# A cached-attention kernel: six batches of x loaded plainly and transposed on TensorE, the other x loads placed behind K loads, constant matmuls at the start, two heads of wq issued by ScalarE

## The chip, the cores and the metric

The kernel runs on one core of a Trainium2 chip. A core has a matrix engine (TensorE, PE in the profile, with PEld for its weight loads), three engines for elementwise work (VectorE or DVE, ScalarE or ACT, GpSimd or POOL), a queue engine (SyncE or SP) that issues transfers, and 16 DMA engines that carry them out. The metric is the device time of one execution in microseconds; the number quoted for a kernel is the median of several executions.

## The reference

Two independent problems, A and B, of the same shape, each an attention block with a given K and V cache:

```python
# x [16, 144, 448]   k_cache, v_cache [16, 16, 512, 256]   wq [448, 4096]   wo [4096, 448]
def _A_ref(x, k_cache, v_cache, wq, wo):
    B, Sq, D = x.shape
    H, Dh = 16, 256
    q = (x @ wq).reshape(B, Sq, H, Dh).transpose(0, 2, 1, 3)
    scores = jnp.einsum("bhqd,bhkd->bhqk", q, k_cache) * (Dh ** -0.5)
    p = softmax(scores, axis=-1)
    o = jnp.einsum("bhqk,bhkd->bhqd", p, v_cache)
    return o.transpose(0, 2, 1, 3).reshape(B, Sq, H * Dh) @ wo
```

`reference` returns the results of A and of B side by side in the last axis. All arrays are bf16.

## The kernel before, in words

A *unit* is one head of one batch; there are 256 in A (units 0 to 255) and 256 in B (256 to 511). The first 32 units take two batches in turn (unit U is head U//2 of batch U%2), after that a batch's 16 heads follow each other. Per unit, TensorE does four things: Q = wq' x' (line 1081; two batches at once for most units), S = K Q (line 1112), PV = V' P (line 1168), and its share of the output projection (line 1284), which is cut into pieces of one 128-row chunk of the output times one of 32 slices of wo. A sum over keys goes through a matmul with ones (line 1184). ScalarE computes the exponentials and the reciprocal of the sum, GpSimd and VectorE add up partial sums, VectorE takes Q out of PSUM (1094, 1095) and scales PV into `ring` (1220), from which the projection reads.

**Steps.** The program of each engine is written out unit by unit in one loop over a step i (from line 1472). At step i stand PV of unit i, S of unit i+2 (i+3 from unit 48 on; function `ls`), Q of one unit more (`lq`), and the projection pieces that `op_schedule` gave to that step. At step 44 the lead changes, so two Q's stand in one step, one right after the other. `_Sched.add` puts in the semaphore waits that reads and writes need; every engine runs its own list in order.

**Projection rate.** `op_schedule` hands out pieces by a credit. There are 2.25 pieces per unit (18 chunks of 32 pieces to 256 units). No piece of A comes before step 28 and none of B before step 272 (`OP_START`); the credit grows by `OP_RATE` times 2.25 per step, 1.04 up to step 272 and 1.15 after it.

**Loads.** x must be on chip transposed (`xt_sb`, a ring of `NX` = 6 batches), K transposed (`kt_sb`, a ring of 32 units), V as it is (`v_sb`, a ring of nine pairs of units). The K of the first 48 units is loaded plainly into the V ring (line 1012, 1017) and transposed on TensorE (`t_tr`, line 1032) with evacuations by VectorE and ScalarE (1040). From unit 48 on, K comes in *waves* of 16 units by one transposing DMA (line 988). x comes by transposing DMAs in groups of one to four batches (`X_GROUPS`, line 964). wq, wo, V and stores are plain DMAs (928 and 930, 939, 1002, 1313). Every DMA is issued by SP, in one order. A planner fixes that order ahead of time: `load_list` gives each load the time at which it is used (`clock`, a sum of TensorE costs per step), the step at which its buffer is free, and a duration; the loop after `todo` then picks loads one by one, and prefers other loads to a K wave if they would fall due during it. The `due` step of a load is where its buffer is free, and SP waits there for the engine that frees it.

The pieces that the change and the steps of the prediction touch: `t_init` (line 899), `t_load_wq` (922), `t_load_x` (944), `t_load_k` (979), `t_evac_op` (1295), `op_schedule` (1327), `load_list` (1394), the planner's loop (1424 to 1456), and the step loop (1459 on).

## Time and profile before

| what | us |
|---|---|
| median of 12 executions | 1055.27 (1053.05 to 1056.87) |
| profiled execution, its own time | 1054.66 |
| its span in the trace (first to last instruction) | 1052.8 |
| TensorE busy in the span | 1029.8 |
| VectorE, ScalarE, GpSimd busy | 737.9, 793.6, 634.7 |
| first matmul starts | 3.60 |
| longest idle time of TensorE inside the span | 6.9, at 595.4 |

The profile page gives busy time and idle time by line; "A <- B" after an idle time names the instruction or transfer whose end let A start. A DMA's row in a timeline shows the time that the issuing engine spent on it, not the transfer; the time to landing is told apart. A group of pipelined matmuls is busy a little longer than the distance to the next group: eight matmuls of 144 columns show 0.66 us and the next group begins 0.50 us after them. In sums the distance is used.

### The profile page before, as it was taken

The page shows a single profiled execution, that of the slowest core. Times are in us where ns is not written, and L with a number is a line of the kernel's source. Part 1 is how long each engine was busy: PE and PEld are TensorE (multiplying, and loading weights), DVE is VectorE, ACT ScalarE, POOL GpSimd, SP SyncE. Part 2 cuts the span into 40 slices and gives each one's busy share as a digit, 9 for nine tenths or more (in the row PEclk, how much of TensorE's full clock was granted, in tenths as well). Part 3 has the DMA queues.
Part 4 walks back from the last instruction along what each step waited for, and adds up shares of the span by engine and source line. Part 5 has one row for each costly group of instructions (what it writes and reads, how often), then busy time and mean ns, then how long its engine had stood idle before and what let it go on. Part 6 is the DMA issues. An engine that isn't in the chain of part 4 may idle for free.

```text
span 1052.8 us, 32329 instructions
## 1 busy us (share of the span) xinstructions
PE 1029.8 (98%) x12376; PEld 875.6 (83%) x12376; DVE 737.9 (70%) x2039; ACT 793.6 (75%) x2365; POOL 634.7 (60%) x1030
## 2 busy tenths in 40 slices
PE   6999999999999999999999799999999999999997
PEld 6999888888888888888888688888888888888885
DVE  5776676777777776777776467677776667777775
ACT  5887577777777777777867567787877777788785
POOL 3655556666666666666755456566666666666673
PEclk9999999999999999999999899999999999999999
DMA  9999999999999999999999999999999999999960
GB/s 287 362 340 346 262 303 262 291 290 290 289 290 295 272 260 252 302 289 296 262 290 341 269 268 300 294 268 295 272 275 257 307 249 313 289 274 260 293 205 14
DMA packets 591748, 294.14 MB, mean 279 GB/s; under 512 B 502592, under 2 KB 516768, under 8 KB 591584
## 3 DMA queue, kind: packets, MB, share of 16 engines
q1 hardware_dynamic: 591584, 291.99, 111.0%
q8 instruction: 99, 1.62, 0.6%
q14 instruction: 65, 0.53, 0.2%
HBM read 161.48 MB, written 4.13 MB: 157 GB/s over the span
## 4 chain that ended last, share of the span: by engine, by line
PE 90%; DMA 6%; SPq 1%; ACT 1%; DVE 1%; issue 0%; POOL 0%; ACTq 0%; DVEq 0%
PE s_ps L1112 23%; PE ot_ps L1168 23%; PE qp_ps L1081 22%; PE op_ps L1284 19%; DMA kt_sb<-in_B_k_cache_dram 2%; DMA kt_sb<-in_A_k_cache_dram 2%; PE ot_ps L1184 2%; DMA wq_sb<-in_A_wq_dram 1%; PE qp_ps L1032 1%; PE s_ps L1032 1%; PE qp_ps L1284 1%; ACT rinv_sb L1205 1%; DMA v_sb<-in_B_v_cache_dram 0%; SPq L1002 0%; ACT pt_sb L1122 0%
## 5 line engine op out<-in xcount | busy, mean ns | idle before, releaser
L1132 POOL TENSOR_TENSOR pp_sb<-pt_sb 128x288 f32<-128x288 bf16 x512 | 383.9, 750 | 322.3 <-ACT pt_sb L1122 307.3
L1122 ACT ACTIVATE pt_sb<-s_ps 128x288 bf16<-128x288 f32 x1024 | 364.6, 408 | 183.6 <-PE s_ps L1112 177.3
L1220 DVE TENSOR_TENSOR ring<-ot_ps,rinv_sb 128x288 bf16<-128x288 f32 (+2 forms) x640 | 241.8, 394 | 159.5 <-ACT rinv_sb L1205 154.0
L1112 PE MATMUL s_ps<-qt_sb,kt_sb 128*128 128x144 bf16 x4096 | 341.2, 227 | 8.3 <-DMA kt_sb<-in_B_k_cache_dram 6.9
L1168 PE MATMUL ot_ps<-pt_sb,v_sb 128*128 128x144 bf16 x4096 | 340.7, 226 | 0.4 <-DMA v_sb<-in_B_v_cache_dram 0.4
L1112 PEld LDWEIGHTS s_ps<-qt_sb,kt_sb 128*128 128x128 bf16 x4096 | 288.2, 98 | 60.3 <-issue 7.3
L1205 ACT ACTIVATE rinv_sb<-ln_sb 64x144 f32<-64x144 f32 x928 | 298.2, 321 | 24.4
L1081 PE MATMUL qp_ps<-xt_sb,wq_sb 128*128 128x288 bf16 (+1 forms) x2368 | 302.1, 271 | 2.9 <-DMA wq_sb<-in_A_wq_dram 1.3
L1284 PE MATMUL op_ps<-wo_sb,ring 128*128 128x448 bf16 x1120 | 285.5, 352 | 0.0
L1081 PEld LDWEIGHTS qp_ps<-xt_sb,wq_sb 128*128 128x128 bf16 x2368 | 212.4, 98 | 77.8 <-DVE qt_sb L1094 2.3
L1168 PEld LDWEIGHTS ot_ps<-pt_sb,v_sb 128*128 128x128 bf16 x4096 | 274.7, 98 | 1.2 <-DMA v_sb<-in_B_v_cache_dram 0.6
L1137 POOL TENSOR_TENSOR p_sb<-pp_sb 128x144 f32<-128x144 f32 x464 | 226.6, 488 | 74.3 <-DVE ps_sb L1146 9.5
L1235 DVE TENSOR_REDUCE run_sb<-ot_ps 128x1 bf16<-128x144 f32 x560 | 146.5, 304 | 78.2 <-ACT ln_sb L1192 43.8
L1146 DVE TENSOR_TENSOR ps_sb<-p_sb 64x144 bf16<-64x144 f32 x464 | 156.1, 337 | 45.4 <-POOL p_sb L1137 32.1
L1095 DVE CAST qt_sb<-qp_ps 128x576 bf16<-128x576 f32 x216 | 162.1, 751 | 14.1 <-PE qp_ps L1081 10.5
L1284 PEld LDWEIGHTS op_ps<-wo_sb,ring 128*128 128x128 bf16 x1120 | 93.8, 98 | 20.1
L1192 ACT ACTIVATE ln_sb<-ot_ps 128x144 f32<-128x144 f32 x232 | 67.7, 292 | 33.1 <-PE ot_ps L1184 25.4
L1184 PE MATMUL ot_ps<-ps_sb,ones 128*128 128x144 bf16 x280 | 63.4, 226 | 0.0
L1094 DVE CAST qt_sb<-qp_ps 128x288 bf16<-128x288 f32 x80 | 35.8, 448 | 2.9 <-PE qp_ps L1081 2.6
L1040 ACT ACTIVATE kt_sb<-qp_ps 128x512 bf16<-128x512 bf16 x48 | 29.0, 605 | 6.0 <-PE qp_ps L1032 6.0
L1137 POOL TENSOR_TENSOR ps_sb<-pp_sb 128x144 bf16<-128x144 f32 x48 | 23.4, 488 | 7.3 <-PE ot_ps L1184 0.6
L1184 PEld LDWEIGHTS ot_ps<-ps_sb,ones 128*128 128x128 bf16 x280 | 27.4, 98 | 0.0
(29 smaller groups left out, 153.6 us busy)
## 6 DMA issues: line engine op xcount, KB each, us to landing
v_sb<-in_A_v_cache_dram SPq DMA_DIRECT2D x128, 512.0 KB, 6.9
v_sb<-in_B_v_cache_dram SPq DMA_DIRECT2D x128, 512.0 KB, 7.3
v_sb<-in_A_k_cache_dram SPq DMA_DIRECT2D x22, 512.0 KB, 10.0
out_dram<-ost_sb SPq DMA_DIRECT2D x36, 112.0 KB, 6.2
wo_sb<-in_A_wo_dram SPq DMA_DIRECT2D x8, 448.0 KB, 8.5
wo_sb<-in_B_wo_dram SPq DMA_DIRECT2D x8, 448.0 KB, 8.7
wq_sb<-in_B_wq_dram SPq DMA_DIRECT2D x4, 768.0 KB, 9.8
wq_sb<-in_A_wq_dram SPq DMA_DIRECT2D x3, 768.0 KB, 10.0
```

The source lines that it names most:

```text
L1081: ins = t.matmul(acc, lhsT=wq_sb[:, kc, c0:c0 + 128], rhs=xt_sb[:, kc, xo:xe + 1:max(xe - xo, 1), :], start=(kc == 0), stop=(kc == 3))
L1095: return v.tensor_copy(qt_sb[:, a:b + 1:b - a, :, :], qp_ps[:, :, 0:2 * SQ].rearrange("p e (u q) -> p u e q", u=2))
L1112: ins = t.matmul(s_ps[bank][:, (c % 2) * SQ:(c % 2 + 1) * SQ], lhsT=kt_sb[:, 2 * c + dc, ko:ko + 128], rhs=qt_sb[:, qsl, dc, :], start=(dc ...
L1122: return a.activation(pt_sb[:, psl, 2 * k:2 * k + 2, :].rearrange("p b q -> p (b q)"), s_ps[bank][:, 0:2 * SQ], AF.Exp, scale=DH ** -0.5)
L1132: return g.tensor_tensor(pp_sb[:, :, :], pt_sb[:, psl, 0:2, :], pt_sb[:, psl, 2:4, :], op=ALU.add)
L1137: return g.tensor_tensor(dst, pp_sb[:, 0, :], pp_sb[:, 1, :], op=ALU.add)
L1146: return v.tensor_tensor(ps_sb[p0:p0 + 64, sl, :], p2_sb[0:64, :], p2_sb[64:128, :], op=ALU.add)
L1168: ins = t.matmul(ot_ps[ob][:, dc * SQ:(dc + 1) * SQ], lhsT=v_sb[:, vsl, j, c * DH + dc * 128:c * DH + (dc + 1) * 128], rhs=pt_sb[:, sl, c, ...
L1205: return a.activation(rinv_sb[p0:p0 + 64, sl, :], ln_sb[h0:h0 + 64, :], AF.Exp, scale=-1.0)
L1220: ins = v.tensor_tensor(ring[:, 2 * h:2 * h + 2, r0:r0 + q1 - q0], ot_ps[ob][:, 0:2 * SQ].rearrange("p (c q) -> p c q", c=2)[:, :, q0:q1], ...
L1235: return v.tensor_reduce(run_sb[:, k, j:j + 1], ot_ps[ob][:, 2 * SQ:3 * SQ], axis=AX.X, op=op)
L1284: ins = t.matmul(acc[0:m, 0:D], lhsT=ring[:, c, col0:col0 + m], rhs=wo_sb[:, c, :], start=(c == op_first), stop=(c == op_last))
```

## The change

Six batches of x (A's batches 0 to 5) are no longer loaded by transposing DMAs. Each is loaded plainly as 48 partitions by three rows of 448 (`t_load_xn`) into the last slices of `wo_sb`, which are not yet in use, and transposed by 12 TensorE transposes into the projection's PSUM bank; VectorE and ScalarE copy it from there to `xt_sb` (`t_tr_x`), at steps -4, -3, 20, 21, 23 and 24. The other x loads are in groups of two batches, and the planner puts one directly behind a K wave as soon as its buffer is free. wq of heads 0 and 1 is issued by ScalarE, at the start. TensorE runs 34 matmuls on a constant as its first work. The projection's rate is 1.0 to step 240, 1.35 to step 292, then 1.15. The second Q of step 44 stands behind PV. The planner's durations of K, x and wq loads are changed, as is its first order of loads. The last chunk's evacuation is split between VectorE and ScalarE.

```diff
-    X_GROUPS = ((0, 1), (1, 2), (2, 6), (6, 10), (10, 14), (14, 18), (18, 20), (20, 24), (24, 28), (28, 32))
+    X_GROUPS = tuple((g, g + 2) for g in range(6, NP * Bn, 2))
-    WQ_GROUPS = ((0, 1), (1, 2), (2, 4), (4, 8), (8, 12), (12, 16))
+    WQ_GROUPS = ((2, 4), (4, 8), (8, 12), (12, 16))
+    WARM = 34
-    OP_DELAY, OP_START, OP_RATE = 2, (28, 16), (1.04, 1.15)
-    MARGIN, HOLD = 1.0, 1.0
+    XR, X_AT = 48, {0: -4, 1: -3, 2: 20, 3: 21, 4: 23, 5: 24}
+    OP_DELAY, OP_START, OP_RATE = 2, (28, 16), ((240, 1.0), (292, 1.35), (600, 1.15))
+    MARGIN, HOLD, K_FIX = 1.0, 1.0, 2.4
...
             S.add(ACT, e1, reads=[("scr", 0)], writes=[("scr1", 0)], name="actwarm")
+            t_load_wq(0, 0, 1, ACT)
+            t_load_wq(0, 1, 2, ACT)
...
+            def e3(g):
+                return g.memset(xt_sb[64:128, 3, :, :], 0.0)
+            S.add(DVE, e3, writes=[(("xt", g), g) for g in range(NX)], name="xz")
...
+            def e6(t):
+                ins = None
+                for _ in range(WARM):
+                    ins = t.matmul(op_ps[:, 0:128], lhsT=ones[:, :], rhs=ones[:, :], start=True, stop=True)
+                return ins
+            S.add(PE, e6, reads=[("ones", 0)], writes=[("opp", ("warm", 0))], banks=["op"], name="FAR")
...
+        def x_rows(g):
+            n = SQ // XR
+            c0 = NWO - (NX - g) * n
+            return n, wo_sb[0:XR, c0:c0 + n, :], [(("wo", c // WOG), -1) for c in range(c0, c0 + n)]
+
+        def t_load_xn(g):
+            n, dst, keys = x_rows(g)
+
+            def e(q):
+                return q.dma_start(dst, xs[0][g].rearrange("(t p) d -> p t d", p=XR)).then_inc(sems["xn%d" % g], 16)
+            S.add(SP, e, writes=keys + [(("xn", g), 0)], dma_sem="xn%d" % g, name="xn%d" % g)
+
+        def t_tr_x(g):
+            n, src, keys = x_rows(g)
+            acc = op_ps[:, :].bitcast(BF16)[:, 0:4 * SQ].rearrange("p (c q) -> p c q", c=4)
+
+            def e(t):
+                ins = None
+                for c in range(4):
+                    m = min(128, D - c * 128)
+                    for k in range(n):
+                        ins = t.transpose(acc[0:m, c, k * XR:(k + 1) * XR], src[:, k, c * 128:c * 128 + m],
+                                          ident[0:XR, 0:XR])
+                return ins
+            S.add(PE, e, reads=keys + [(("xn", g), 0), id_key], writes=[("opp", ("x", g))], banks=["op"], name="TX%d" % g)
+
+            def e1(v):
+                return v.tensor_copy(xt_sb[:, 0:3, g, :], acc[:, 0:3, :])
+            S.add(DVE, e1, reads=[("opp", ("x", g))], writes=[(("xt", g), g)], banks=["op"], name="exd%d" % g)
+
+            def e2(a):
+                return a.activation(xt_sb[0:64, 3, g, :], acc[0:64, 3, :], AF.Copy)
+            S.add(ACT, e2, reads=[("opp", ("x", g))], writes=[(("xt", g), g)], banks=["op"], name="exa%d" % g)
...
+            parts = ((ACT, 0, D),) if eng == ACT else ((DVE, 0, D // 2), (ACT, D // 2, D))
+            for eng, c0, c1 in parts:
+                def e(g, eng=eng, c0=c0, c1=c1):
+                    if eng == ACT:
+                        return g.activation(ost_sb[0:m, sl, c0:c1], acc[0:m, c0:c1], AF.Copy)
+                    return g.tensor_copy(ost_sb[0:m, sl, c0:c1], acc[0:m, c0:c1])
...
-                credit += OP_RATE[i >= NU + OP_START[1]] * NCH * NWO / NU
+                credit += next(r for u, r in OP_RATE if i < u) * NCH * NWO / NU
...
-                load(first_q[g0], (g1 - NX) * H - lq(NT) if g1 > NX else s_min, 1.3 + 0.55 * (g1 - g0), t_load_x, XG)
+                load(first_q[g0], (g1 - NX) * H - lq(NT) if g1 > NX else s_min, 2.0 + 0.55 * (g1 - g0), t_load_x, XG)
...
-                load(u0 - ls(u0), last - ls(last) + 1 if last >= 0 else s_min, 2.0 + 0.97 * (u1 - u0), t_load_k, W)
+                load(u0 - ls(u0), last - ls(last) + 1 if last >= 0 else s_min, K_FIX + 0.97 * (u1 - u0), t_load_k, W)
...
-                    load(first_h[pr, h0], NU - H + h1 - lq(NU) if pr else s_min, 0.65 * (h1 - h0), t_load_wq, pr, h0, h1)
+                    load(first_h[pr, h0], NU - H + h1 - lq(NU) if pr else s_min, 0.78 * (h1 - h0), t_load_wq, pr, h0, h1)
...
+            for g in X_AT:
+                load(X_AT[g], s_min, 0.4, t_load_xn, g)
...
-        first = [(t_load_n, (0, 0)), (t_load_x, (0,)), (t_load_wq, (0, 0, 1)), (t_load_n, (0, 1))]
+        first = [(t_load_xn, (0,)), (t_load_n, (0, 0)), (t_load_n, (0, 1)), (t_load_xn, (1,))]
...
+            after_k = len(dma_plan) and dma_plan[-1][0] is t_load_k
...
+                if after_k and m[3] is t_load_x and start <= now:
+                    best = (start, latest, m, lo)
+                    break
...
-            now += m[2] - (1.0 if m[3] is t_load_k and dma_plan and dma_plan[-1][0] is t_load_k else 0.0)
+            now += m[2] - (1.4 if after_k and m[3] in (t_load_k, t_load_x) else 0.0)
...
+            for g in X_AT:
+                if X_AT[g] == i:
+                    t_tr_x(g)
...
-            for u in of_step(lq, i):
+            for u in of_step(lq, i)[:1]:
                 if q_pair(u):
                     t_q(u)
                     t_evac_q(u)
...
                 t_pv(u)
                 if u < P0 or u % 2 == 0:
                     t_sum(u)
+            for v in of_step(lq, i)[1:]:
+                if q_pair(v):
+                    t_q(v)
+                    t_evac_q(v)
```

More of the change, by code (lines that the diff above doesn't have):

```diff
@@ L868, in bass_concat_heads__mha_block_cached__gqa_block_cached__near_ridge_kernel @@
             sem_names.append("n%d" % i)
+        for i in range(NX):
+            sem_names.append("xn%d" % i)
         for i in range(NWG):
@@ L920, in t_init, with t_load_wq @@
             S.add(POOL, e5, reads=[("ones", 0)], writes=[id_key], name="ident")
-        def t_load_wq(pr, h0, h1):
+        def t_load_wq(pr, h0, h1, eng=SP):
             cols = slice(h0 * DH, h1 * DH)
@@ L930, in e @@
                 return q.dma_start(wq_sb[0:64, 3, cols], w[384:448, cols]).then_inc(sems[sem], 16)
-            S.add(SP, e, writes=[(("wq", h), pr) for h in range(h0, h1)], dma_sem=sem, n_dma=2,
+            S.add(eng, e, writes=[(("wq", h), pr) for h in range(h0, h1)], dma_sem=sem, n_dma=2,
                   name="wq%d.%d" % (pr, h0))
@@ L1299, in t_evac_op @@
             key = "opp" if bank == "op" else "qp"
-            if eng == ACT:
-                def e(a):
-                    return a.activation(ost_sb[0:m, sl, :], acc[0:m, 0:D], AF.Copy)
-            else:
-                def e(v):
-                    return v.tensor_copy(ost_sb[0:m, sl, :], acc[0:m, 0:D])
-            S.add(eng, e, reads=[(key, ("o", r))], writes=[(("ost", sl), r)], banks=[bank], name="eop%d" % r)
+            parts = ((ACT, 0, D),) if eng == ACT else ((DVE, 0, D // 2), (ACT, D // 2, D))
[4 more added lines that the diff above has]
+                    return g.tensor_copy(ost_sb[0:m, sl, c0:c1], acc[0:m, c0:c1])
+                S.add(eng, e, reads=[(key, ("o", r))], writes=[(("ost", sl), r)], banks=[bank], name="eop%d" % r)
         def t_store(r):
```

## The prediction

> **What bounds the kernel now.** I read the page first.
>
> ```profile
> span 1052.8 us, 32329 instructions
> PE 1029.8 (98%) x12376; PEld 875.6 (83%) x12376; DVE 737.9 (70%) x2039; ACT 793.6 (75%) x2365; POOL 634.7 (60%) x1030
> PE   6999999999999999999999799999999999999997
> DMA  9999999999999999999999999999999999999960
> ```
>
> TensorE is busy 98% of the span, so only its 23 us of idle time and its slow matmuls can be won; and the DMA engines are nearly as full, so a stage with extra loads can run dry. The waits of TensorE say where:
>
> ```profile
> PE s_ps L1112 <- DMA kt_sb<-in_B_k_cache_dram: 6.9, 1, 6.9
> PE s_ps L1032 <- DMA v_sb<-in_A_k_cache_dram: 6.0, 2, 3.6
> PE qp_ps L1081 <- DMA wq_sb<-in_A_wq_dram: 1.3, 1, 1.3
> PE qp_ps L1081 <- DVE qt_sb L1094: 0.9, 1, 0.9
> PE s_ps L1112 <- DMA kt_sb<-in_A_k_cache_dram: 0.6, 1, 0.6
> ```
>
> Columns: total, times, longest. The largest is one wait for a K wave of B. TensorE's timeline there, then windows over it (busy by engine, granted clock, DMA):
>
> ```profile
> 594.87 0.54 PE L1284 MATMUL op_ps<-wo_sb,ring 128*128 128x448 bf16 x2
> 602.31 1.12 PE L1112 MATMUL s_ps<-qt_sb,kt_sb 128*128 128x144 bf16 x8 [6.90 <-DMA kt_sb<-in_B_k_cache_dram]
> 603.22 1.17 PE L1168 MATMUL ot_ps<-pt_sb,v_sb 128*128 128x144 bf16 x8
> ```
>
> ```profile
> 594.50:598.00 3.50, 0.91 (x11) 0.47 (x8) 1.86 (x6) 1.95 (x6) 1.21 (x2) 1.00 1.53 240
> 598.00:602.30 4.30, 0.00 (x0) 0.02 (x1) 0.00 (x0) 0.00 (x0) 0.00 (x0) 0.50 0.88 208
> 605.00:608.20 3.20, 3.20 (x24) 2.76 (x23) 1.11 (x3) 0.82 (x2) 0.72 (x2) 0.50 1.05 401
> ```
>
> The wait costs twice: 6.9 us of idleness, and the granted clock falls to 0.50 at 598.0 and stays there to 608.2, so eight matmuls take 1.12 us for 0.66. Against each matmul's usual distance, TensorE loses 9.8 us there. The chain of waits names the transfer:
>
> ```profile
> 576.86 25.31 DMA kt_sb<-in_B_k_cache_dram
> 602.17 0.14 issue
> ```
>
> It was not slow, it was late. From 501.25 to 602.17 transfers land without a hole: three K waves (16.5, 18.3 and 17.5 us after what landed before them), B's wq (14.6 together), B's wo (9.5), 17 V pairs (24.0) and two stores (0.6), together 100.9. The start:
>
> ```profile
> 3.60 0.61 PE L1032 MATMUL s_ps<-qt_sb,v_sb 128*128 128x128 bf16 x4 [3.60 <-DMA v_sb<-in_A_k_cache_dram]
> 7.03 0.59 PE L1032 MATMUL s_ps<-qt_sb,v_sb 128*128 128x128 bf16 x4 [2.40 <-DMA v_sb<-in_A_k_cache_dram]
> 7.41 1.16 PE L1081 MATMUL qp_ps<-xt_sb,wq_sb 128*128 128x144 bf16 x8
> 10.39 0.91 PE L1112 MATMUL s_ps<-qt_sb,kt_sb 128*128 128x144 bf16 x8
> ```
>
> TensorE waits 3.6 us, then 2.4, and runs at half rate to 10.9 (a Q takes 1.16 us here, 0.66 from 11.6 on; the clock column shows 1.00 here, the durations are what to trust). By 25 us it has lost 10.7 us, counted from the span's start.
>
> **The change part by part.** The profiled execution took 1054.66 us, 1.8 over its span and 0.6 under the median of 1055.27; gains are summed from its rows and taken off the median.
>
> *The start.* SP now issues in turn, with the landing: K of unit 0 (0.81, 3.55), x0 (1.26, 4.21), wq of head 0 (2.63, 5.64), K of unit 1 (3.87, 6.90). The first ten instructions end at 7.8 us; a transposing x issue takes 1.32 and 1.22 us, a plain one 0.4 to 0.6. The change issues x0, K0, K1, x1 plainly: K1 goes out at about 1.9 and lands near 4.8. ScalarE's four wq issues cost it 4 x 0.55 = 2.2 us, from 1.0 (beside its table load) or 2.5 us (behind it), done by 3.2 to 4.7, before its first copy. Two memsets change nothing: VectorE's new one, by its neighbour (4096 columns in 1.76 us, so 864 in 0.4), ends by 3.6. The 34 constant matmuls start behind `ones` (1.0 us) and last 34 x 0.10 = 3.4 (half rate: groups of four begin 0.40 apart at 3.60) or 34 x 0.056 = 1.9, so they end at 2.9 to 4.6, while x0 lands about 3.6: a loss of up to 1 us there. Then come transposes of x0, TR of unit 0, x1, TR of unit 1, Q, and S of unit 0. With a mixed clock: 4.5 + 0.7 + 0.7 + 0.5 + 0.3 + 0.7 to Q's end, 7.4, and 1.6 more (Q to S is 3.0 at half rate, half of that at full): S at 9.0 for 10.39. All at full rate from 3.6 on (0.3, 0.5, 0.3, 0.2, 0.5, then 1.5) gives 6.9; at half rate throughout from 4.6 (1.2, 0.9, 1.2, 0.5, 1.0, then 3.0), 12.4. The crossing's clock came back 5.9 us after work resumed at 602.3, which here would be 6.9, so I take the middle. From S on the clock is open: 0.25 us more. The wait for wq at 24.1 (1.3 us) should go, since SP is some 3.5 us ahead in a stretch where windows show 183 GB/s in the first 10 us against 358 in the next. Together +2.9 (-2.0 to +5.0).
>
> A rule against the second issuer: the Trainium skill, "DMA: Bandwidth & Descriptors", section "Issuing engines are not separate DMA queues", says several issuing engines save only the sequencers' issue time, usually small beside the transfer. That is the row's own reading here, where issue is what limits; taken as "small", the rule would leave the start at +1 and the total 1.9 us later. The skill's "TensorE: Matmul & The Clock Gate", Part 4, says transposes do not count as busy for the clock; by it the 24 early transposes would not help to open the clock, and S would stand near 10. The 20 transposes between 7.0 and 11.4 cannot settle that, as matmuls stand among them.
>
> *Transposes of batches 2 to 5*, 48 instructions on a TensorE that has no idle time between 25 and 112 us. Nearest row: a transpose of 128 columns begins 0.056 us after the last. These move 48 columns; 144, 288 and 448 columns take 0.063, 0.123 and 0.190, a line that gives 0.022 for 48 if the weight load (128 wide as before) allows. Between them 0.040: -1.9 (-1.1 to -2.7). Their copies (VectorE 0.42 x 432/512 = 0.35, ScalarE 0.31 each) lie beside 78% and 85% busy engines with Q three steps away: nothing, and 0.3 us a batch if that cover were gone. Their plain loads sit ahead of A's wo in the same buffer, so SP could wait for step 24 with V behind it; V leads by up to 18 units: nothing.
>
> *Step 44.* At 112 the second Q waits for the first's evacuation, 1.1 us between them beyond their work. Behind PV that is covered, but now the next step's Q follows it after two projection pieces (0.38) where 0.65 of evacuation is needed: +0.8 (0.4 to 1.1). The wave that is 0.8 late at 116.6 (0.65 of it named a wait) may be issued earlier, as the planner counts less for x: +0.4 (0 to 0.8).
>
> *The crossing from A to B.* S of unit 288 stands at step 285; the K wave whose issue opens the hole-free stretch is released at step 237, at 497.11. From there TensorE needs 98.3 us to be ready (595.41), the DMA engines 105.1. Counting pieces: 494 done by step 237 and 608 by step 285, so 114. At rate 1.0 from step 28 the new kernel has done 4 + 209 x 2.25 = 474 by 237, and by 285 6.8 + 45 x 3.04 more, 617: 143. So 29 pieces x 0.19 = 5.5 us more work lies in the stretch. The waits for V at 561 (0.6) and two hiccups (0.6) go: 98.3 + 5.5 - 1.1 = 102.7. On the other side, the groups of two put x of batches 20 and 21 behind the second of the three waves: free at step 252, the wave at 253. Four batches behind a wave landed 2.9 after it, so 1.4: 106.5. All wo and V of the stretch are used before step 286, so reordering cannot spare them. Left: 3.8 us of idleness for 6.9. The clock fell 2.6 us into the old wait, so I let it fall again and cost 2.0 for 2.9. Gain: 9.8 - 5.8 and the 0.6 at 561 less 0.4 for x behind the earlier wave: +4.2 (0 to +10.4).
>
> *Between*, pieces only move in time: nothing. Per 16 units TensorE now needs 16 x 1.53 + 36 x 0.19 = 31.3 us, the DMA engines 17.2 for K, 8 x 1.35 for V, 0.4 and 0.7 for stores and x: 29.1. SP, which has the K issue for 18 us, gets an x issue of 1.6 to 3.6 behind it and V behind that: covered by the 2.2 us.
>
> *The end.* The last copy takes 0.62 on VectorE, with ScalarE idle; halves take 0.37: +0.25. POOL issues nothing new.
>
> Sum: 2.9 - 1.9 + 0.8 + 0.4 + 4.2 + 0.25 = 6.65, so 1048.6.
>
> **The rivals.**
> *The K wait goes altogether.* The planner now counts longer K and wq loads and may order them better, or the stretch may open earlier. Another 3.8 and 2.0 us go: 1042.8. Against it: a full DMA stretch of 105 us whose content I cannot shorten.
> *The K wait stays as it is*, the extra pieces being eaten by x loads or by an order with more V ahead of the wave: 6.65 - 4.2 = 2.45, so 1052.8. For it: the planner puts everything that falls due ahead of K.
> *Slower: the DMA engines become the bound in A.* With less projection up to step 240 and an x load behind waves, each of 12 waves could be late. To lose the 6.65 and 2.1 more, each must lose 0.73 us, that is need 32.0 us per 16 units in place of 29.1: V pairs at 1.7 us would do it. A few land after 1.9 to 2.8, most after 1.35, and SP waits for TensorE before nearly every wave (326 us in all), so I hold it unlikely: 1057.5 or above.
>
> **How the numbers follow.** What a measurement here can tell from no change is about 0.2%, 2.1 us. Forecast 0.45 (1046 to 1051.5), wait gone 0.27, wait unchanged 0.15, slower 0.10, the rest for less mishap. Faster 0.81: the first two, most of the third and some of the rest; same 0.09; slower 0.10. The range, 1041 to 1055, cuts the slower case and the best start together with no wait.
>
> **What would show it.** The first matmul near 1.1 us and S of unit 0 near 9; 72 transposes 0.04 apart; no wait at step 44; TensorE's wait for B's K at 3 to 4 us, with or without a clock of 0.50 behind it. It is wrong if that wait is zero or still 7, or if new waits for K or V stand between 120 and 500 us.

## The result and the profile after

The changed kernel takes 1067.00 us (median of 7 runs, 1062.84 to 1067.75) against 1055.11 us for the kernel before (28 runs beside them): the ratio is 1.0109, with a 95% interval of 1.0099 to 1.0119. It is slower by 1.1%, where the prediction said 1048.6 us. The profiled execution took 1065.57 us with a span of 1063.8, so 11.0 us of span more than before. The line numbers below are those of the changed kernel; the same work stands some 50 lines further down (S is L1163, PV is L1219, the projection L1335, the transposes of x L1017).

The page of the changed kernel, its first lines and two of its strips:

```profile
span 1063.8 us, 32561 instructions
PE 1039.0 (98%) x12482; PEld 880.9 (83%) x12482; DVE 742.8 (70%) x2046; ACT 794.8 (75%) x2372; POOL 635.0 (60%) x1030
...
PE   8999999999999999999997999999999999999997
...
DMA  9999999999999999999999999999999999999950
```

TensorE is as full as before, and the one weak slice in the middle is still there, a little earlier (before it was the one at 595 us, now it is the one behind 558 us). What changed is what TensorE waits for. Its waits in the changed kernel (total, times, longest):

```profile
PE ot_ps L1219 <- DMA v_sb<-in_B_v_cache_dram: 11.7, 5, 5.7
PE op_ps L1017 <- DMA wo_sb<-in_A_x_dram: 2.4, 1, 2.4
PE s_ps L1163 <- DMA kt_sb<-in_A_k_cache_dram: 1.9, 1, 1.9
PE ot_ps L1219 <- DMA v_sb<-in_A_v_cache_dram: 1.1, 2, 0.7
...
PE s_ps L1163 <- DMA kt_sb<-in_B_k_cache_dram: 0.4, 1, 0.4
```

The wait for B's K, 6.9 us before, is down to 0.4. In its place stands a wait for V, 11.7 us in five places of B, and a wait of 2.4 us at the start. The longest wait for V, in TensorE's timeline, and windows over it (busy by engine, granted clock, DMA):

```profile
565.46 0.66 PE L1163 MATMUL s_ps<-qt_sb,kt_sb 128*128 128x144 bf16 x8
571.80 1.14 PE L1219 MATMUL ot_ps<-pt_sb,v_sb 128*128 128x144 bf16 x8 [5.68 <-DMA v_sb<-in_B_v_cache_dram]
```

```profile
562.00:566.00 4.00, 4.00 (x54) 3.38 (x51) 2.71 (x8) 3.04 (x10) 1.90 (x3) 1.00 1.11 251
566.00:568.80 2.80, 0.12 (x2) 0.00 (x0) 0.72 (x2) 0.67 (x2) 1.80 (x4) 1.00 0.93 196
568.80:575.60 6.80, 3.80 (x19) 2.47 (x20) 0.98 (x3) 0.93 (x3) 0.00 (x0) 0.50 1.05 381
```

It is the old picture with another tile: 5.7 us of idleness, and behind it a clock of 0.50 for 6.8 us. SyncE's queue shows why V is late there. First the changed kernel, then the kernel before (start, length of the issue, what is issued):

```profile
537.71 26.73 SPq L1039 DMA_TRANSPOSE kt_sb<-in_B_k_cache_dram  x1
564.48 1.31 SPq L981 DMA_TRANSPOSE xt_sb<-in_B_x_dram  x1
565.83 1.60 SPq L1053 DMA_DIRECT2D v_sb<-in_B_v_cache_dram  x3
```

```profile
530.12 26.82 SPq L988 DMA_TRANSPOSE kt_sb<-in_B_k_cache_dram  x1
556.99 2.12 SPq L1002 DMA_DIRECT2D v_sb<-in_B_v_cache_dram  x4
```

The K wave's issue holds SyncE for 27 us in both. In the changed kernel the whole group starts 7.6 us later, and a pair of x stands between K and V. K lands at 567.07, x at 568.21, the first V pair at 571.76; before, K landed at 559.85 and V at 561.25, 1.4 us behind it and not 4.7.

Where the 11.0 us of span went, counted as in the prediction (each matmul's distance to the next against its usual distance, transposes of x and constant matmuls counted as loss; before minus after, so a gain is positive):

| stretch of the span, us | before | after | gain |
|---|---|---|---|
| 0 to 25 (start) | 10.7 | 10.7 | 0 |
| 25 to 100 (transposes of batches 2 to 5) | -0.5 | 2.3 | -2.8 |
| 100 to 125 (step 44, K of unit 48) | 1.8 | 2.3 | -0.5 |
| 125 to 550 | -0.5 | 1.4 | -1.9 |
| 550 to 625 (crossing) | 10.3 | 8.3 | +2.0 |
| 625 to the end | -0.4 | 7.6 | -8.0 |

(Each stretch is taken in its kernel's own time. The rounded rows sum to -11.2; the span says -11.0.)

### The profile page after: what moved, and what is told of

It is laid out like the page before. It is cut to its first block, busy times and chain, and to the rows that moved or that the text cites. A ratio compares the mean times of both kernels' runs of the same rounds, so it can differ in the third digit from the quotient of the medians.

```text
span 1063.8 us, 32561 instructions
## 1 busy us (share of the span) xinstructions
PE 1039.0 (98%) x12482; PEld 880.9 (83%) x12482; DVE 742.8 (70%) x2046; ACT 794.8 (75%) x2372; POOL 635.0 (60%) x1030
## 4 chain that ended last, share of the span: by engine, by line
PE 89%; DMA 8%; SPq 1%; ACT 1%; DVE 0%; issue 0%; POOL 0%; ACTq 0%; DVEq 0%
PE ot_ps L1219 22%; PE s_ps L1163 22%; PE qp_ps L1132 22%; PE op_ps L1335 18%; DMA kt_sb<-in_B_k_cache_dram 2%; DMA v_sb<-in_B_v_cache_dram 2%; DMA kt_sb<-in_A_k_cache_dram 2%; PE ot_ps L1235 2%; PE s_ps L1083 1%; PE qp_ps L1083 1%; DMA v_sb<-in_A_v_cache_dram 1%; SPq L981 1%; PE qp_ps L1335 1%; DMA wo_sb<-in_A_x_dram 0%; PE op_ps L1017 0%; ACT rinv_sb L1256 0%
## 5 line engine op out<-in xcount | busy, mean ns | idle before, releaser
L1219 PE MATMUL ot_ps<-pt_sb,v_sb 128*128 128x144 bf16 x4096 | 340.2, 226 | 12.8 <-DMA v_sb<-in_B_v_cache_dram 11.7
L1163 PE MATMUL s_ps<-qt_sb,kt_sb 128*128 128x144 bf16 x4096 | 340.5, 226 | 2.8 <-DMA kt_sb<-in_A_k_cache_dram 1.9
L1163 PEld LDWEIGHTS s_ps<-qt_sb,kt_sb 128*128 128x128 bf16 x4096 | 287.3, 98 | 55.7 <-DVE qt_sb L1146 6.2
L1335 PE MATMUL op_ps<-wo_sb,ring 128*128 128x448 bf16 x1120 | 286.6, 354 | 0.0
L1219 PEld LDWEIGHTS ot_ps<-pt_sb,v_sb 128*128 128x128 bf16 x4096 | 274.0, 98 | 14.6 <-DMA v_sb<-in_B_v_cache_dram 6.7
L1188 POOL TENSOR_TENSOR p_sb<-pp_sb 128x144 f32<-128x144 f32 x464 | 226.6, 488 | 74.9 <-DVE ps_sb L1197 10.5
L1197 DVE TENSOR_TENSOR ps_sb<-p_sb 64x144 bf16<-64x144 f32 x464 | 159.3, 343 | 45.2 <-POOL p_sb L1188 31.6
L1335 PEld LDWEIGHTS op_ps<-wo_sb,ring 128*128 128x128 bf16 x1120 | 93.9, 98 | 20.4 <-issue 0.4
```

What stands on the lines that cost most here:

```text
L1163: ins = t.matmul(s_ps[bank][:, (c % 2) * SQ:(c % 2 + 1) * SQ], lhsT=kt_sb[:, 2 * c + dc, ko:ko + 128], rhs=qt_sb[:, qsl, dc, :], start=(dc ...
L1188: return g.tensor_tensor(dst, pp_sb[:, 0, :], pp_sb[:, 1, :], op=ALU.add)
L1197: return v.tensor_tensor(ps_sb[p0:p0 + 64, sl, :], p2_sb[0:64, :], p2_sb[64:128, :], op=ALU.add)
L1219: ins = t.matmul(ot_ps[ob][:, dc * SQ:(dc + 1) * SQ], lhsT=v_sb[:, vsl, j, c * DH + dc * 128:c * DH + (dc + 1) * 128], rhs=pt_sb[:, sl, c, ...
L1335: ins = t.matmul(acc[0:m, 0:D], lhsT=ring[:, c, col0:col0 + m], rhs=wo_sb[:, c, :], start=(c == op_first), stop=(c == op_last))
```

## The experiments

Two readings stood against each other after this. **The order of the loads:** the rule that puts a pair of x straight behind a K wave delays every V behind it, the DMA queue has no idle time to win it back, and the lead so lost comes out as waits in B. **The other parts:** groups of two in place of four, the new projection rate, or the new start with its transposes cost the time by themselves. Within the first, a narrower question follows further down, whether a pair costs only where it stands or draws on a lead; each expectation spells out the theories that it means. Ratios are to the kernel before, timed beside each kernel on the same chip; it took 1054.07, 1053.71 and 1054.54 us in the three series of experiments and 1055.11 beside the changed kernel. Differences between kernels of different series are therefore given by medians and, where it matters, by ratios. The lead of a V pair is the time from its landing to the start of the PV that uses it; leads come from one profiled execution of each kernel.

### x loaded as before

```
-    X_GROUPS = tuple((g, g + 2) for g in range(6, NP * Bn, 2))
+    X_GROUPS = ((6, 10), (10, 14), (14, 18), (18, 20), (20, 24), (24, 28), (28, 32))
...
-                if after_k and m[3] is t_load_x and start <= now:
-                    best = (start, latest, m, lo)
-                    break
```

> The changed kernel (1067.0 us), with the x loads from batch 6 on in the groups of before (four batches) and picked by due time, not behind a K wave. Theory X: an x load behind a K wave costs the DMA engines 1.1 us and then 2.2 more until the next V lands, 13 times over, and that made V late in B: without it the waits for V at 566, 702, 764 and 824 us shrink and the time falls by 7 to 10 us, to 1057 to 1060. Theory R: the projection's new rate took away the lead of the DMA engines in A, so V is late in B whatever the x loads do: 1064 to 1067.

Measured: 1052.30 us (10 runs, 1049.83 to 1059.57), ratio 0.9994 (0.9973 to 1.0015). V's lead is back: V of unit 128 lands 14.5 us ahead of its use, where it was 14.2 before the change and 9.1 after it. The time lies below both ranges of the expectation. So at the new projection rate the 1.1% come from the later x loads, from their size or their place.

### Pairs of x, but by due time

Only the rule goes; the pairs stay.

```
-                if after_k and m[3] is t_load_x and start <= now:
-                    best = (start, latest, m, lo)
-                    break
```

> The changed kernel with x in pairs, but picked by due time, not behind a K wave. Separates the size of the groups from their place. If the place costs (no x in the transfers of B's crossing when it is picked late): near the kernel with the old groups, 1051 to 1056. If the pairs cost (13 turns from plain to transposing loads in place of seven): 1060 to 1066.

Measured: 1051.11 us (5 runs, 1049.56 to 1054.83), ratio 0.9976 (0.9956 to 0.9997). So the size of the groups costs nothing, and at the new rate three lines of the planner cost 1067.0 - 1051.1 = 15.9 us by the medians, 14.0 by the ratios. The rule does not reach all pairs: in the changed kernel 8 of the 13 pairs are issued directly behind a wave (three in A, from 117 us on, and five in B), the other five ahead of one. The waits of the kernel without the rule:

```profile
PE op_ps L1017 <- DMA wo_sb<-in_A_x_dram: 3.2, 1, 3.2
PE s_ps L1163 <- DMA kt_sb<-in_A_k_cache_dram: 1.7, 1, 1.7
PE ot_ps L1219 <- DMA v_sb<-in_B_v_cache_dram: 1.3, 3, 0.8
```

V in B is down from 11.7 to 1.3 us, none long enough to cost the clock. Its queue at the crossing, for comparison with the two above:

```profile
531.28 24.49 SPq L1039 DMA_TRANSPOSE kt_sb<-in_B_k_cache_dram  x1
555.81 1.60 SPq L1053 DMA_DIRECT2D v_sb<-in_B_v_cache_dram  x3
```

No x stands there, and the wave is issued 6.4 us earlier than in the changed kernel.

### The rule in A alone, and from batch 14 on alone

```
-                if after_k and m[3] is t_load_x and start <= now:
+                if after_k and m[3] is t_load_x and start <= now and X_GROUPS[m[4][0]][0] < 14:
```

> After, with the pick behind a K wave for the first four pairs of x only (batches 6 to 13, loaded in A between 110 and 230 us); the later pairs are chosen by due time. With no pick at all it was 1051.1, with all of them 1067.0. Theory one (lead: each pair behind a wave takes some 2 us of V's lead in A, and it is never won back, because the DMA queue has no idle time): V's lead at unit 128 is 9 to 10 us, as in after, the crossing into B uses it up, TensorE waits 3 to 6 us for V between 555 and 620 us, and the time is 1055 to 1061. Theory two (each pair costs only in the place where it stands, and in A the lead covers it): lead back at 13 by unit 240, no wait for V over 1 us in B, 1050 to 1053.

Measured: 1057.70 us (12 runs, 1053.63 to 1060.70), ratio 1.0024 (1.0009 to 1.0038), so 6.6 us over no rule at all by the medians, 5.1 by the ratios. V's lead is 9.8 us at unit 128 and still 10.2 at unit 240: what the pairs took in A (three of the four stand behind a wave) does not come back. The wait in the crossing is one for K, where I had written one for V:

```profile
607.51 1.12 PE L1163 MATMUL s_ps<-qt_sb,kt_sb 128*128 128x144 bf16 x8 [3.17 <-DMA kt_sb<-in_B_k_cache_dram]
```

K and V share one queue, so which of them is caught is a matter of their order; the 1.12 us for eight matmuls shows the halved clock again. Not all of this execution's loss is the rule's. The transposes of batch 3 wait for a plain load of x, and the clock is at 0.50 from 60.60 to 64.02 us, before any pair of x stands behind a wave:

```profile
59.98 0.58 PE L1017 MATMUL op_ps<-qt_sb,wo_sb 48*128 48x48 bf16 x12 [1.78 <-DMA wo_sb<-in_A_x_dram]
60.84 1.17 PE L1132 MATMUL qp_ps<-xt_sb,wq_sb 128*128 128x144 bf16 x8
```

That is 3.3 us more between 25 and 100 us than in the kernel without the rule. Batch 3 itself had landed at 54.17 us; the load that ended the wait, at 59.85, is that of batch 4, whose slices share a group with batch 3's (more on these groups below). In the changed kernel batch 4 landed at 57.44, 0.37 us ahead of batch 3's transposes.

With ">= 14" in place of "< 14":

> After, with the pick for the pairs from batch 14 on only; the first four are chosen by due time. Theory one: lead of 14 us at unit 128 and some 12 at 240; the pair of batches 20 and 21 in the crossing and the three in B after it still cost 2 to 4 us each where the lead is near zero, so 1056 to 1062, and this and the run with the first four alone share the 16 us. Theory two: all of the 16 us, 1063 to 1068. If the first pairs are what decides, 1050 to 1053.

Measured: 1060.55 us (6 runs, 1056.93 to 1063.64), ratio 1.0050 (1.0033 to 1.0067), so 9.4 us over no rule by the medians, 7.8 by the ratios. The lead is 14.7 us at unit 128 and 11.8 at 240, and the waits stand in B:

```profile
PE ot_ps L1219 <- DMA v_sb<-in_B_v_cache_dram: 6.1, 4, 3.3
...
PE s_ps L1163 <- DMA kt_sb<-in_B_k_cache_dram: 4.3, 1, 4.3
```

6.6 and 9.4 make 16.0 for the 15.9 of both together (by the ratios 12.9 for 14.0). So there is not one bad place. The sum does not tell a lead that is drawn down from pairs that each cost something where they stand, since these would add up too, and both profiled executions hold a wait of batch 3's transposes that is not the rule's (1.3 us in this one). For a lead speaks the kernel with the rule in A alone: no pair of x stands in its crossing, and yet TensorE waits there.

### The rule on the kernel before

The pairs and the rule are put into the old kernel; all else stays.

```
-    X_GROUPS = ((0, 1), (1, 2), (2, 6), (6, 10), (10, 14), (14, 18), (18, 20), (20, 24), (24, 28), (28, 32))
+    X_GROUPS = ((0, 1), (1, 2), (2, 6)) + tuple((g, g + 2) for g in range(6, NP * Bn, 2))
...
+                if after_k and m[3] is t_load_x and start <= now:
+                    best = (start, latest, m, lo)
+                    break
```

> The kernel before (1055.1 us) with one part of the change: x from batch 6 on in pairs, each picked directly behind a K wave. Theory X: waits for V appear in B as in the changed kernel, 1060 to 1065. Theory R: within 1.5 us of before, 1054 to 1056.5.

Measured: 1058.65 us (4 runs, 1058.54 to 1060.17), ratio 1.0047 (1.0030 to 1.0064). The rule costs the old kernel 4.6 us, and puts the same kind of wait in the same place:

```profile
564.15 0.67 PE L1168 MATMUL ot_ps<-pt_sb,v_sb 128*128 128x144 bf16 x8 [2.50 <-DMA v_sb<-in_B_v_cache_dram]
```

This lies between the ranges of the two theories. The wait for K in the crossing stays (7.3 us), and V's lead in A does not fall: 14.2 us at unit 128 and 14.0 at unit 240, for 14.2 and 13.4 before. The rule costs less here than in the changed kernel; the next experiments show that the new start alone does not make the difference, and that the new rate does beside it.

### The projection rate as before, alone and with x as before

```
-    OP_DELAY, OP_START, OP_RATE = 2, (28, 16), ((240, 1.0), (292, 1.35), (600, 1.15))
+    OP_DELAY, OP_START, OP_RATE = 2, (28, 16), ((272, 1.04), (600, 1.15))
```

> The changed kernel with the projection's rate of before (1.04 to step 272, then 1.15). Theory X: V is as late as in the changed kernel, and the wait for K of unit 288 comes back: 1066 to 1070. Theory R: V leads by 9 us or more again before step 240 and the waits for V in B go: 1056 to 1060.

> The changed kernel with both the x groups and picks of before and the rate of before; what stays of the change is the start, the six plain batches and the planner's durations. If the new rate is worth the 4.2 us at the crossing that the prediction gave it, this is 4 to 7 us slower than the same kernel with the new rate (1052.3): 1056 to 1059, with a wait for K of unit 288 of 5 us or more. If the rate is worth nothing once the DMA engines set the pace there: 1051 to 1054.

Measured: with the rule in place, 1064.63 us (4 runs, 1064.19 to 1066.00; ratio 1.0098, 1.0081 to 1.0115), 2.4 us less than with the new rate by the medians, 1.2 by the ratios, whose intervals overlap: the new rate brings nothing there, and whether it costs anything is not shown. With x as before, 1062.82 us (4 runs, 1060.81 to 1063.72; ratio 1.0081, 1.0064 to 1.0098) against 1052.30, so the new rate is worth 10.5 us (9.2 by the ratios). The waits for B's K and V, of the kernel with the rule and then of the one with x as before:

```profile
PE s_ps L1163 <- DMA kt_sb<-in_B_k_cache_dram: 12.7, 2, 11.4
...
PE ot_ps L1219 <- DMA v_sb<-in_B_v_cache_dram: 0.8, 1, 0.8
```

```profile
PE s_ps L1163 <- DMA kt_sb<-in_B_k_cache_dram: 11.5, 2, 9.9
```

Without the rule, the projection work put into the crossing does what the prediction wanted of it, and more: it takes away a wait for K of 10 us, and with it a clock of 0.50 for 10.2 us, from 604.5 on.

Neither theory of the first kernel holds whole. V is not late in it (0.8 us for 11.7), and its lead is 13.0 us at unit 128 and 13.4 at unit 240, as theory R had it; but the wait for K comes back, as theory X had it, and the time hardly moves. The four kernels with the new start, by median:

| | rate as before | new rate |
|---|---|---|
| x as before | 1062.82 | 1052.30 |
| pairs, with the rule | 1064.63 | 1067.00 |

At the rate of before the rule costs 1.8 us, which is within the intervals; at the new rate it costs 14.7 (12.1 by the ratios). So most of its price is that it takes the new rate's gain away again. The table shows one thing more: with x and rate as before, the rest of the change (start, plain batches, the planner's durations) is itself 0.81% slower than the kernel before. Its span is 7.9 us longer, of which 3.4 lie between 550 and 650 us, where it waits 11.5 us for K and not 6.9, and 2.5 in the transposes of batches 2 to 5. Which of these parts makes that wait longer was not taken apart.

### The new rate on the kernel before

```
-                credit += OP_RATE[i >= NU + OP_START[1]] * NCH * NWO / NU
+                credit += next(r for u, r in OP_RATE if i < u) * NCH * NWO / NU
```

(with the new triple of rates in place of the two).

> The kernel before with the new projection rate alone. By the prediction's working the wait for K of unit 288 falls from 6.9 us by 5.5 to 1.4 (no pair of x lies in the stretch here) and the clock stays up: 1046 to 1049. If the rate only moves the wait (the transfers between units 256 and 384 take about 299 us whatever TensorE does, and V's lead at step 240 shrinks with A's lower rate): waits for V at 300 to 390 take its place, 1052 to 1056.

Measured: 1051.26 us (9 runs, 1048.93 to 1051.99), ratio 0.9969 (0.9959 to 0.9979). The wait for K at unit 288 is gone altogether; but the planner now puts the second wave ahead of B's last wq, and a Q waits:

```profile
556.81 2.08 PE L1081 MATMUL qp_ps<-xt_sb,wq_sb 128*128 128x288 bf16 x8 [4.47 <-DMA wq_sb<-in_B_wq_dram]
```

A gain of 2.4 us, between the two ranges; the rest is eaten by the new wait, behind which the clock is at 0.50 for 3.4 us.

### x of each plain batch in slices of its own

The plain loads of x borrow rows of wo's buffer. The slices of batches 0 and 1 share one group of wo, and with it one key of the dependency list, so the transposes of batch 0 wait for the load of batch 1 too. Here each batch gets a group.

```
-            c0 = NWO - (NX - g) * n
+            c0 = (2 + g) * WOG
```

> The changed kernel with each of the six plainly loaded batches in a slice group of wo of its own, so that the transposes of batch 0 no longer wait for the load of batch 1 (the two share a group in the changed kernel). The transposes of batch 0 should begin at 4.9 us in place of 7.3 and S of unit 0 at about 10.3 in place of 12.7. If TensorE's start passes through to the end: 1064.5. If the DMA engines set the pace later (waits for V at 566 us and after), the 2.4 us are given back there: 1066.5 to 1067.

Measured: 1060.17 us (7 runs, 1057.15 to 1065.23), ratio 1.0069 (1.0049 to 1.0090). The changed kernel's start, then this one's:

```profile
1.06 3.81 PE L930 MATMUL op_ps<-ones 128*128 128x128 bf16 x34 [1.06 <-POOL ones L924]
7.32 0.80 PE L1017 MATMUL op_ps<-qt_sb,wo_sb 48*128 48x48 bf16 x12 [2.45 <-DMA wo_sb<-in_A_x_dram]
...
12.72 0.66 PE L1163 MATMUL s_ps<-qt_sb,kt_sb 128*128 128x144 bf16 x8
```

```profile
4.80 0.82 PE L1017 MATMUL op_ps<-qt_sb,wo_sb 48*128 48x48 bf16 x12
8.21 0.80 PE L1017 MATMUL op_ps<-qt_sb,wo_sb 48*128 48x48 bf16 x12 [1.62 <-DMA wo_sb<-in_A_x_dram]
12.11 1.17 PE L1163 MATMUL s_ps<-qt_sb,kt_sb 128*128 128x144 bf16 x8
```

The wait for x1 (which landed at 7.18 in the changed kernel, where x0 had landed at 3.33) moves from batch 0's transposes to batch 1's, which stand ahead of S of unit 0. The false dependence is shown; alone it moves S by 0.6 us. The gain in time, 6.8 us by the medians and 4.2 by the ratios, is larger than that and below both ranges of the expectation. Its waits in B:

```profile
PE ot_ps L1219 <- DMA v_sb<-in_B_v_cache_dram: 5.0, 4, 1.7
PE s_ps L1163 <- DMA kt_sb<-in_B_k_cache_dram: 4.2, 1, 4.2
```

Against 11.7 and 0.4 that is 2.9 us less waiting, and the clock is at 0.50 for 3.4 us in place of 10.2. V's lead at unit 128 is 11.1 us for 9.1. The list of loads is the same in both kernels, so these 2 us come from the start or from one execution to the next; which of them was not taken apart. The same false dependence ties batch 3 to batch 4, and made the waits of 1.8 and 1.3 us at 58 to 60 us that stand further up.

### x as before and one constant matmul

x as before (the first experiment), and

```
-    WARM = 34
+    WARM = 1
```

> The changed kernel with the x loads of before from batch 6 on, and one constant matmul in place of 34. TensorE then waits for x of batches 0 and 1 without having worked. If the 34 matmuls open the clock early: S of unit 0 is 0.5 to 1.5 us later than with them and the clock opens 1 to 3 us later, 1053 to 1054.5. If the wait of 2.4 to 2.9 us behind them throws that away: no difference, 1051.5 to 1053.

Measured: 1059.46 us (10 runs, 1052.15 to 1062.13), ratio 1.0041 (1.0020 to 1.0061), against 1052.30 with 34. In the profiled execution, which is the shortest of the ten, S of unit 0 begins at 13.5 us for 12.9 with 34, and no wait over 2 us follows. The clock opens for good at 14.5 us, and at 15.3 with 34, where it had been open from 5.1 to 8.5, mostly over the wait. The ten runs lie in two clumps, four at 1052 to 1054 and six at 1059 to 1062, and the clump that makes the median has no profile. With 34 the runs spread as far (1049.83 to 1059.57), but two of ten lie above 1058. Where the 7 us of the upper clump are lost stays open, and so does whether the constant matmuls are worth anything.

### A version that beats both

Pairs by due time, slices of their own, and batch 1's transposes one step later:

```
-    XR, X_AT = 48, {0: -4, 1: -3, 2: 20, 3: 21, 4: 23, 5: 24}
+    XR, X_AT = 48, {0: -4, 1: -2, 2: 20, 3: 21, 4: 23, 5: 24}
```

> After, with pairs by due time, x of each plain batch in wo slices of its own and the transposes of batch 1 one step later, so that neither they nor those of batch 0 wait for x1. Against 1051.1 with pairs by due time alone: the transposes of batch 0 begin at 4.8 for 8.3 and S of unit 0 at 10 to 11 for 12.7 to 13; 1047.5 to 1049.5. If the start is bound by wq of head 1 (7.6) and the half clock instead, S of unit 0 stays at 12 and the time at 1050 to 1051.

Measured: 1048.71 us (6 runs, 1048.49 to 1053.03), ratio 0.9957 (0.9940 to 0.9973). Its start:

```profile
4.74 0.59 PE L1017 MATMUL op_ps<-qt_sb,wo_sb 48*128 48x48 bf16 x12
...
7.39 0.59 PE L1017 MATMUL op_ps<-qt_sb,wo_sb 48*128 48x48 bf16 x12
...
9.29 0.66 PE L1163 MATMUL s_ps<-qt_sb,kt_sb 128*128 128x144 bf16 x8
```

S of unit 0 begins at 9.29 us, for 10.39 before the change and 12.72 after it. The median is 2.4 us below the 1051.11 with the shared group, but the intervals of the two ratios overlap, so this gain is likely and not shown. Then the first K wave one place earlier in the list, ahead of the V pair before it:

```
+        j = next(n for n, p in enumerate(dma_plan) if p[0] is t_load_k)
+        dma_plan.insert(j - 1, dma_plan.pop(j))
+        due.insert(j - 1, due.pop(j))
```

> The same, and the first K wave (for units 48 on) issued one place earlier, ahead of the V pair before it. If the 1.9 us wait at 119 us is that wave's place in the queue (a V pair is 1.35 us), it shrinks to 0.3 to 0.6 and the time is 1.4 us less than without. If V for the units before it is late in its place, no gain.

Measured: 1048.05 us (6 runs, 1045.45 to 1051.85), ratio 0.9945 (0.9929 to 0.9960). S of unit 48 no longer waits for K:

```profile
116.67 0.73 PE L1163 MATMUL s_ps<-qt_sb,kt_sb 128*128 128x144 bf16 x8 [0.25 <-ACT pt_sb L1173]
```

The wait, 1.8 us without this step, is gone and K lands 2.3 us ahead. S of unit 0 begins at 10.32 here, with the same start: the clock opened at 6.34 us and not at 4.60, and TensorE waited 1.1 us for K. Between the two versions the medians differ by 0.7 us with runs that overlap, so that this step's gain in time is likely but not shown. Both versions are faster than the old kernel, by 0.4 to 0.6%, and than the changed one.

## Why the prediction was wrong

**"Between, pieces only move in time: nothing" is the step that failed.** Two numbers in it were wrong.

*What the DMA engines need per 16 units.* The prediction had 29.1 us against TensorE's 31.3 and called the 2.2 us between them cover. In the changed kernel V of unit 128 and V of unit 240 land 216.9 us apart, which is 31.0 per 16 units, and their uses lie 217.1 us apart, 31.0 too. There is next to no cover: V's lead is 9.1 us at one end and 9.2 at the other, and in between the DMA engines stand without a packet for 1.1 us in all, which is 0.16 per 16 units. The 1.9 us come from V (mean 1.5 us between two V pairs, where I had taken the median of 1.35, so 1.2 for eight), from K (a wave takes 19.15 us from the transfer ahead of it to the V behind it, which less 1.35 is 17.8 for my 17.2), and the rest from x.

*What a pair of x behind a wave costs.* The prediction took 1.4 us in the crossing and 0.7 per 16 units elsewhere. From the last transfer ahead of a wave to the first V behind it, the changed kernel takes 19.15 us with K alone (median of 15) and 21.47 with a pair behind it (median of 8, 20.4 to 23.5): 2.3 us, and 4.4 in the crossing. By due time it is not free either: 20.6 us with the pair ahead of the wave (3 cases), and 2.45 for 1.35 where it stands among V pairs (the middle of 4 cases between 2.4 and 4.0). Against these places (1.6 and 1.1 us a pair, each by its own kernel's waves) the rule costs some 0.7 to 1.2 us a pair, and it moves pairs to an earlier wave.

Neither alone would make 14 to 16 us. After the same content (14 K waves, 7 pairs, all of B's wq), the V pair for unit 266 lands at 548.2 us in the changed kernel and at 541.6 with pairs by due time. Of these 6.6 us, groups that hold K or x account for 4.9; the rest is spread over gaps between plain loads, and why those are longer I can't say. In the crossing an eighth pair (batches 20 and 21) comes ahead of the next V, which is the wait at 566; the V pair for unit 286 lands at 593.8 for 583.5. The lead is gone at unit 268 (0.0 us), and three more pairs behind waves, at 684, 744 and 805 us, are each followed by a wait for V, at 702, 764 and 824. Two of the waits halve the clock, for 6.8 and 3.4 us.

How much of the crossing's loss is lead, and how much the pairs that stand in it, can be read off the kernels (one profiled execution each; the loss counted as in the table above):

| kernel | V's lead at units 128, 240 | pairs behind waves between 540 and 600 us | lost 550 to 650 |
|---|---|---|---|
| new rate: pairs by due time | 14.6, 13.7 | 0 | -0.5 |
| new rate: x as before | 14.5, 12.3 | 0 | 0.8 |
| new rate: x as before, one constant matmul | 11.8, 9.5 | 0 | 2.3 |
| new rate: rule in A alone | 9.8, 10.2 | 0 | 4.5 |
| new rate: rule from batch 14 on | 14.7, 11.8 | 2 | 7.0 |
| new rate: own slices | 11.1, 10.9 | 2 | 7.0 |
| new rate: changed kernel | 9.1, 9.2 | 2 | 8.1 |
| rate as before: x and rate as before | 14.8, 10.9 | 0 | 13.8 |
| rate as before: rule kept | 13.0, 13.4 | 2 | 15.9 |
| kernel before | 14.2, 13.4 | 0 | 10.4 |
| kernel before, with the rule | 14.2, 14.0 | 2 | 12.3 |

At the new rate a low lead alone costs 3 to 5 us, two pairs in the crossing at a better lead 6 to 8, and both together 7 to 9. So both count and they do not simply add up; single executions can't tell more. At the rate of before the rule takes less than 2 us of lead and costs 2 us, since K is late there with or without it. The prediction's "V leads by up to 18 units: nothing" reads a lead as cover. It is a stock: with a queue as slow as its user it is spent once. But at unit 128 the lead was below 11.5 us only where the rule met the new rate, at which TensorE needs 31.0 us per 16 units between units 128 and 240 and not 31.3, and in the crossing a lead of 9.5 us without the rule made no wait for V over 1.0 us.

**The rivals.** The one with the DMA engines as the bound in A was held unlikely because 32.0 us per 16 units were wanted for it. Its mechanism is what happened, at 31.0 us; the point from which it decides was wrong, since equality is enough once something draws the lead down. And the loss shows in B, 300 us and more behind the pairs of A. "SP waits for TensorE before nearly every wave" was evidence read the wrong way: SyncE waits for a slot in the K buffer while its queue still holds work, and between V of unit 128 and V of unit 240 the DMA engines have only three gaps over 0.15 us, the longest 0.57.

**The start, +2.9: measured 0.** S of unit 0 began at 12.72 us and not at 9.0; what it lost, the rest of the first 25 us gave back: the wait for wq at 24.1 (1.3 us) is gone as predicted, and so are shorter waits for other engines. The step that failed is "x0 lands about 3.6" followed by its transposes: they wait for x1 as well, 2.45 us, and the clock stays at half until 12.47 us. With the false dependence away and batch 1's transposes one step later, S begins at 9.29 in one version and at 10.32 in the other, where the prediction's clocks allowed 6.9 to 12.4. ScalarE's four issues were done by 3.2 us, as counted.

**Transposes of batches 2 to 5, -1.9: right.** The rows after, each a group of 12 and the next instruction:

```profile
55.17 0.59 PE L1017 MATMUL op_ps<-qt_sb,wo_sb 48*128 48x48 bf16 x12
55.70 0.40 PE L1083 MATMUL s_ps<-qt_sb,v_sb 128*128 128x128 bf16 x4
```

12 in 0.53 us are 0.044 each for 0.040, so 2.1 us; the stretch loses 2.8. The rows show no wait for their copies, as predicted. What the term left out is the shared group of batches 3 and 4: with the rule in A alone it cost 3.3 us at 58 to 64 us.

**Step 44, +0.8 and +0.4: one right, one of the wrong sign.** The wait between the two Q at 112 us went from 1.1 to 0.34. K of unit 48 came later, not earlier: its issue follows a V issue that waits for a slot, and that came at 98.21 us for 96.01 before, as the PVs, which free the slots, ran 2.2 us later (that of unit 37 began at 98.02 for 95.82). The wait went from 0.8 to 2.0 us; moving the wave ahead of that V issue ends it.

**The crossing, +4.2: measured +2.0, by another road.** Its core was right: more projection work in the stretch takes the wait for K from 6.9 us to 0.4, where I left 3.8. What came in its place was the wait for V (5.7 us and the clock). Without the pairs of x in the crossing (pairs by due time) nothing is lost there, which is the best case that the prediction allowed for it (+10.4).

**The end, +0.25: wrong sign, -0.15.** The halves of the last copy were to run side by side. Before, then after:

```profile
1047.52 0.62 DVE L1305 CAST ost_sb<-qp_ps 128x448 bf16<-128x448 f32 x1 [2.44 <-PE qp_ps L1284]
1048.17 0.33 SPq L1313 DMA_DIRECT2D out_dram<-ost_sb  x1
```

```profile
1058.51 0.39 DVE L1356 CAST ost_sb<-qp_ps 128x224 bf16<-128x224 f32 x1 [2.45 <-PE qp_ps L1335]
1058.93 0.36 ACT L1355 ACTIVATE ost_sb<-qp_ps 128x224 bf16<-128x224 f32 x1 [2.16 <-DVE ost_sb L1356]
1059.31 0.33 SPq L1364 DMA_DIRECT2D out_dram<-ost_sb  x1
```

ScalarE waits for VectorE, because both halves write under one key; the store goes out 0.80 us behind the copy's start for 0.65.

The forecast of 1048.6 us is met by the version without the rule and with the false dependence removed (1048.71). That is partly chance, since its crossing gains more and its K of unit 48 less than the terms had it; and its part behind 650 us loses 3.3 us more than before; but the order of the loads, with the start a smaller part, is what lay between the forecast and the result.

## What to carry to other kernels

Where transfers land with next to no gap, measure the queue's pace from landing to landing over a long stretch before calling the difference to the consumer cover, and use means, not medians: a lead of 14 us that nothing refills would pay for six pairs at 2.3 us and no more, and the wait then appears far behind the place that caused it. Try a change in each of the company it will keep: the rule cost 2 to 5 us beside one rate and 12 to 16 beside the other. Put small loads that are due late behind the loads that are due now, even where the order looks cheaper for the queue. Where a step is expected to start early or two halves to run side by side, look at the keys by which dependencies are kept: two of the terms failed on a key that covered more than the data.

## What the runs showed of the hardware

- The issue of one K wave, a transposing load, holds SyncE's queue for 18 us in A at 99 us and for 26.7 us in the crossing; the next issue on that queue follows within 0.05 us of its end in both (at 117.12 and 564.48).
- A transposing load of x directly behind a transposing load of K takes 2.0 to 2.3 us more until the next V has landed (3 cases with pairs by due time, 8 in the changed kernel), against 1.1 us among V loads and 1.6 ahead of the wave (4 and 3 cases, pairs by due time).
- The clock fell 2.7 us after the start of the wait of 5.7 us at 566.1, 2.8 us after that of the wait of 2.1 us at 702.6 (when the wait was over and TensorE had work again), 2.4 us after that of the wait of 1.8 us at 58.2 with the rule in A alone (over too), and 4.3 us after that of the wait at 552.3 in the old kernel with the new rate. It stayed at half for 6.8, 3.4, 3.4 and 3.4 us, and for 10.2 us in the kernel with x and rate as before. The Trainium skill, "TensorE: Matmul & The Clock Gate", Part 1, has the clock decided over freely running windows of about 3.4 us; the spells here, one, two and three times 3.4 us, agree. By it a wait's price depends on where in a window it falls.
- The 34 constant matmuls (1.06 to 4.9 us) did not open the clock for good where a wait for x followed. In the changed kernel, with 2.45 us of idleness behind them, half rate lasts to 12.47 us, and with own slices, where transposes follow at once and a wait of 1.62 us behind these, to 13.8. In four others (x as before, with either rate; rate as before; rule from batch 14 on) the clock was at full from 3.8 to 5.1 us on, for 3.4 us that the wait mostly took, and then at half for 6.8. It stayed open in the two versions with no wait over 1 us behind the constants: from 4.60 us, where 12 transposes at 4.74 take 0.52 us, and from 6.34 us in the twin with the early K wave, where they take 0.75 us at 4.81.
